# Token blocks of 512 in place of a batch's halves of 288 in the middle of a fused attention and two-layer chain

## The chip, the cores and the metric

The kernel runs on one core of a Trainium2 chip. The metric is the device time of one execution in microseconds (us), lower is better. TensorE (PE) multiplies, VectorE (DVE), ScalarE (ACT) and GpSimd (POOL) work elementwise, and SyncE (SP) issues the transfers. Every matmul is preceded by a load of its stationary operand, which the profile shows on a row of its own (PEld).

## What is computed

Four batches of eight heads attend over 576 tokens with a window of 128 and a bias that falls with distance; the result, 2304 tokens of width 512, goes through two layers:

```python
scores = scale * np.matmul(q, k.transpose(0, 1, 3, 2))
scores = np.where(mask, scores + bias[None], -1000000000.0)
attn = np.exp(scores - np.max(scores, axis=-1, keepdims=True))
attn = attn / (np.sum(attn, axis=-1, keepdims=True) + 1e-09)
x = np.matmul(attn, v)                  # as 2304 x 512
h = (x @ w1) * (x @ w2) @ w3            # w1, w2: 512 x 1024, w3: 1024 x 1024
y = h @ w_out                           # 1024 x 512
h = y @ w_in                            # 512 x 2048
out = (h * np.clip(h + 3.0, 0.0, 6.0) / 6.0) @ w_out2   # 2048 x 512
```

## The kernel before, in words

Every large product is made of three matmuls (`mm3`, lines 46 to 48): each operand is split into a high and a low part, and high by high, high by low and low by high are summed in PSUM. `split` (L74 on ACT, L75 on the engine given) makes the parts.

**Attention.** Heads go in 16 pairs `n`, four to a batch. A pair is cut into six slots (`attn_slot`): `products` (L144, the tile `s`), `scores` (L168 on DVE, L177 on ACT), `normalize` (L185, L186 on DVE, L193 on POOL), `pt` (L217, L221: transpositions of the probabilities `pr`), `pv` (L238, the tile `X`), then `x_parts`, which copies X to `xf` (L245) and splits it into `xh` and `xl`. There are two sets of `qw`, `kw`, `vw` and of four `pr` tiles, used by pairs in turn, so that a pair's loads (L113, L114, L117, all on SP's queue) come up to two pairs ahead.

**ab and y.** w3 and w_out are multiplied into one matrix W during the first 100 us. Then the tokens of a batch `b` go in two halves `s` of 288: eight `ab_unit` (f = 0 to 7; two PSUM banks, 12 triples of matmuls in all for w1 and w2, `asb` copied by ACT at L467, multiplied by DVE at L470, split into `g`), and four `y_unit` (d = 0 to 3; 8 triples over f). A half's 12 units are 8 x 24 + 4 x 24 = 288 matmuls, each 288 columns wide. y's halves are the two token halves of a scheme that needs fewer products: `y_unit` stores seven combinations to DRAM (`yT`, L489): Y11, Y21, Y22 and the differences t1 to t4.

Slots of attention are put between the units: after unit number `done` the slots up to `nslot + done + 3` have been issued. A scheduler that simulates the engines sets the final order from this program order; instructions in `keep_in_program_order` stay where they are.

**h and o.** In three blocks `j` of 384 token pairs, eight weight pairs `p` each: `h_pair` makes seven products (384 columns wide), gates them (`gate`: L659, L660, L74, L75) into `g2` tiles, and `o_jobs` adds four groups of three o matmuls (512 wide) into six PSUM banks. After the last weight pair the banks are copied out (L734 on ACT, L736 on DVE) and stored (L527). Since a block of 384 isn't a multiple of 288, `rows` cuts a 128-token store at the border of a half: 24 stores in all.

**Pools.** `xpool`, `wpool`, `sp` and `gp` lie in that order on the left side of SBUF and are closed at the end of y; `vA`, `vL`, `r2` and `g2p` then take their room. On the right, attention's tiles give way to `dec` (raw words of weights, two buffers), `vR` and `yrp` (three buffers for y read back).

The second layer's weights come as packed words, are unpacked and split on ACT and DVE (`va_make`, `vo_make`), stored to DRAM (`vad`, `vod`) and fetched again in later blocks. The first six are made during the last batch (`AT`), at whose end y's seven combinations for j = 0 are read back (`y_load`) and split (`y_split`).

Of the kernel before, what the change touches and what calls it, by code (L numbers as in the profile page):

```python
# [22 lines left out]
def tile_attention_moe_moe2(ctx: ExitStack, tc: tile.TileContext, qT, kT, vm, vt, wo, w3, w12, w2x, out):  # L23
# [56 lines left out]
    relm = cpool.tile([P, 2 * P], F32, name="relm")  # L80
# [15 lines left out]
    a1 = apool_ctx.enter_context(tc.tile_pool(name="a1", bufs=1, side="right"))  # L96
    raw_ctx = ExitStack()
# [6 lines left out]
    qw = [a1.tile([P, S + P - TAIL], F32, name=f"qw{i}") for i in range(2)]  # L104
    kw = [a1.tile([P, S], F32, name=f"kw{i}") for i in range(2)]
    vw = [a1.tile([P, NC, P], F32, name=f"vw{i}") for i in range(2)]
    rel8 = a1.tile([P, H, 2 * P], BF16, name="rel8")
    prt = [a1.tile([P, 2 * P], F32, name=f"prt{i}") for i in range(2)]

    def load_hp(n, names):  # L110
        for nm in names:
            if nm == "v":
                nc.sync.dma_start(out=vw[n % 2][:, 0 : NC - 1, :], in_=vm[n])  # L113
                nc.sync.dma_start(out=vw[n % 2][0:TAIL, NC - 1, :], in_=vt[n])  # L114
            else:
                r, src = (qw, qT) if nm == "q" else (kw, kT)
                nc.sync.dma_start(out=r[n % 2][:, 0:S], in_=src[n])  # L117
# [34 lines left out]
    def scores(n, j):  # L152
# [9 lines left out]
        pr = prt[n % 2] if tail else a1.tile([P, 2, 2 * P], F32, tag=f"pr{n % 2}", bufs=4, name=f"pr_{n}_{j}")  # L162
# [66 lines left out]
    def pv(n):  # L229
# [14 lines left out]
        x = a1.tile([P, S], F32, tag="xf", name=f"xf_{n}")  # L244
        nc.scalar.copy(x, X[:, 0:S])  # L245
        x_parts(n, x)

    def x_parts(n, x):
        xs[n] = []
        for s in range(2):  # L250
            nb = NP + 1 if s == 0 else 2 * NP - 1
            xh = xpool.tile([P, HS], F32R, tag=f"xh{s}", bufs=nb, name=f"xh_{n}_{s}")
            xl = xpool.tile([P, HS], F32R, tag=f"xl{s}", bufs=nb, name=f"xl_{n}_{s}")
            split(xh, xl, x[:, s * HS : (s + 1) * HS], nc.vector if n == NP - 1 else nc.gpsimd)
            xs[n].append((xh, xl))
# [3 lines left out]
    def attn_slot(g):  # L259
# [12 lines left out]
        if s == 1:  # L272
            normalize(n, (0, 1))
            if 0 < n < NHP - 1:
                load_hp(n + 1, "v")
# [180 lines left out]
    def ab_unit(b, s, f):  # L456
        pss = []
        hi, lo = wsp[f]
        for k in range(2):
            ps = bank(b, f"ab{k}_{b}_{s}_{f}")  # L460
            for c in range(KD):
                xh, xl = xs[b * NP + c][s]
                mm3(ps[:, 0:HS], hi[:, k * KD + c, :], lo[:, k * KD + c, :], xh, xl, c == 0, c == KD - 1)
            pss.append(ps)
            if k == 0:
                asb = xpool.tile([P, HS], F32, tag="asb", bufs=2, name=f"asb_{b}_{s}_{f}")
                nc.scalar.copy(asb, ps[:, 0:HS])  # L467
        g = gp.tile([P, 2, HS], F32R, tag="g", name=f"g_{b}_{s}_{f}")
        gh, gl = g[:, 0, :], g[:, 1, :]
        nc.vector.tensor_tensor(out=asb, in0=pss[1][:, 0:HS], in1=asb, op=ALU.mult)  # L470
        split(gh, gl, asb, nc.vector)
        gt[b, s, f] = (gh, gl)
# [4 lines left out]
    def y_unit(b, s, d):  # L477
        ds_ = slice(d * P, (d + 1) * P)
        ps = bank(b, f"y_{b}_{s}_{d}")
        for f in range(KF):  # L480
            gh, gl = gt[b, s, f]
            mm3(ps[:, 0:HS], W["h"][:, f, ds_], W["l"][:, f, ds_], gh, gl, f == 0, f == KF - 1)
        ci = d % 2

        def new(tag):
            return sp.tile([P, HS], F32, tag=tag, bufs=1, name=f"{tag}_{b}_{s}_{d}")

        def put(t, k):
            nc.sync.dma_start(out=yT[ci, k, :, b * HS : (b + 1) * HS], in_=t)  # L489

        if s == 0:
            ys[d] = new(f"y0{d}")
            nc.scalar.copy(ys[d], ps[:, 0:HS])
            put(ys[d], Y11 if d < 2 else Y21)
        elif d < 2:
            ys["t", ci] = new(f"t1{ci}")
            nc.vector.tensor_tensor(out=ys["t", ci], in0=ps[:, 0:HS], in1=ys[ci], op=ALU.subtract)
            put(ys["t", ci], YT1)
        else:
            y22, t2, t3, t4 = (new(t) for t in ("y22", "t2", "t3", "t4"))  # L500
            nc.scalar.copy(y22, ps[:, 0:HS])  # L501
            put(y22, Y22)
            nc.vector.tensor_tensor(out=t2, in0=y22, in1=ys["t", ci], op=ALU.subtract)
            put(t2, YT2)
            nc.vector.tensor_tensor(out=t3, in0=t2, in1=ys[ci], op=ALU.subtract)
            put(t3, YT3)
            nc.vector.tensor_tensor(out=t4, in0=t2, in1=ys[d], op=ALU.subtract)
            put(t4, YT4)
# [11 lines left out]
    place = {p: n for n, p in enumerate(FIRST)}  # L520
# [46 lines left out]

    yraw = {}
    yc = {}

    def y_load(j, i):
        k = PRODUCTS[i][1]
        yraw[j, i] = yrp.tile([P, 2, TH], F32, tag="yr", name=f"yraw{j}_{k}")
        dma(yraw[j, i], yT[:, k, :, j * TH : (j + 1) * TH].rearrange("c p t -> p c t"))

    def y_split(j, i):
# [5 lines left out]
        if i + 3 < len(PRODUCTS):  # L582
# [3 lines left out]
    units = []  # L586
    for s in range(2):
        units += [("ab", s, f) for f in range(KF)] + [("y", s, d) for d in range(KD)]
    g = nslot
    for b in range(B):  # L590
        if b == B - 1:
# [6 lines left out]
            yrp = ctx.enter_context(tc.tile_pool(name="yrp", bufs=3, side="right"))  # L598
# [249 lines left out]
```

## Time and profile before

| what | value |
|---|---|
| time, median of 3 runs | 874.26 us (871.99 to 876.93) |
| the profiled execution's own time | 873.87 us |
| its span, first to last instruction | 872.1 us |
| PE busy | 847.9 us (97%), 5264 matmuls |
| PEld busy | 744.3 us (85%) |
| DVE, ACT, POOL busy | 462.8, 383.6, 97.9 us |
| granted TensorE clock | 0.999 of full speed |

The span has four stages: up to about 101 us the first batch's attention and W; 101 to 386 us ab and y with the attention of the other batches between them; 386 to 484 us ab and y alone, with decoding on ACT and DVE; from 484 us h and o. Spans of matmuls overlap, since they are pipelined: how fast they go is read from the distance of their starts.

### The profile page before, as it was taken

The numbers are of one execution on the slowest core, as the hardware profiler recorded it, in microseconds if no ns is written. First come the engines' busy times: TensorE is split into PE (matmuls) and PEld (weight loads), VectorE is DVE, ScalarE is ACT, GpSimd is POOL, SyncE is SP. The second block draws the span as 40 slices with busy tenths as digits, with TensorE's granted clock in tenths as the row PEclk, the third lists the DMA queues.
The fourth block names the chain that finished last, engine by engine and source line by source line (L and its number), as shares of the span: only waits on it lengthen the run. The fifth ranks groups of instructions, "written<-read, shape, count | busy, mean of one in ns | idle before, by whom it ended". The sixth has DMA issues, their size and how long they took to land.

```text
span 872.1 us, 13688 instructions
## 1 busy us (share of the span) xinstructions
PE 847.9 (97%) x5264; PEld 744.3 (85%) x5264; DVE 462.8 (53%) x1074; ACT 383.6 (44%) x859; POOL 97.9 (11%) x188
## 2 busy tenths in 40 slices
PE   5999999999999999999999899999999999999997
PEld 3454699899898989999999888989889888898886
DVE  5896652444414444232667787786644346443443
ACT  6676653443424344331555454554433235332322
POOL 3314222220222222020000000000000000000000
PEclk9999999999999999999999999999999999999999
DMA  9973211112101120006477779569865558645402
GB/s 362 362 289 133 90 42 62 49 42 96 52 33 41 54 96 15 28 1 219 172 277 269 271 259 361 200 250 381 297 248 200 199 196 308 225 176 223 181 1 72
DMA packets 37393, 148.99 MB, mean 171 GB/s; under 512 B 4049, under 2 KB 17617, under 8 KB 26065
## 3 DMA queue, kind: packets, MB, share of 16 engines
q1 hardware_dynamic: 37328, 148.13, 46.8%
q8 instruction: 41, 0.67, 0.3%
q14 instruction: 24, 0.19, 0.1%
HBM read 112.07 MB, written 36.04 MB: 170 GB/s over the span
## 4 chain that ended last, share of the span: by engine, by line
PE 90%; DVE 4%; DMA 3%; issue 1%; POOL 1%; ACT 1%; SPq 0%; DVEq 0%; POOLq 0%; ACTq 0%
PE ab L46 8%; PE o L46 8%; PE o L47 8%; PE o L48 7%; PE ab L47 7%; PE ab L48 7%; PE wps L350 7%; PE h L46 7%; PE h L47 6%; PE h L48 6%; PE y L46 4%; PE y L47 4%; PE y L48 4%; PE X L238 3%; PE pt L217 3%; PE s L144 2%
## 5 line engine op out<-in xcount | busy, mean ns | idle before, releaser
L46 PE MATMUL ab<-xh,w12h 128*128 128x288 f32 x512 | 156.4, 306 | 0.4 <-ACT y L501 0.3
L47 PE MATMUL ab<-xl,w12h 128*128 128x288 f32 x512 | 151.2, 295 | 0.0
L48 PE MATMUL ab<-xh,w12l 128*128 128x288 f32 x512 | 150.8, 295 | 0.0
L46 PE MATMUL h<-yhi,va 128*128 128x384 f32 x336 | 114.2, 340 | 1.4 <-issue 1.1
L46 PE MATMUL o<-vo,g 128*128 128x512 f32 x288 | 113.1, 393 | 1.4 <-ACT g L74 1.4
L47 PE MATMUL h<-ylo,va 128*128 128x384 f32 x336 | 113.3, 337 | 0.8 <-DVE ylo L75 0.8
L48 PE MATMUL h<-yhi,va 128*128 128x384 f32 x336 | 113.2, 337 | 0.0
L47 PE MATMUL o<-vo,g 128*128 128x512 f32 x288 | 113.1, 393 | 0.0
L46 PEld LDWEIGHTS ab<-xh,w12h 128*128 128x128 f32 x512 | 96.2, 188 | 9.1 <-issue 6.5
L47 PEld LDWEIGHTS ab<-xl,w12h 128*128 128x128 f32 x512 | 96.6, 189 | 0.2 <-issue 0.2
L48 PEld LDWEIGHTS ab<-xh,w12l 128*128 128x128 f32 x512 | 96.4, 188 | 0.0
L48 PE MATMUL o<-vo,g 128*128 128x512 f32 x288 | 86.5, 392 | 0.0
L659 ACT ACTIVATE rl<-c,three 128x384 f32<-128x384 f32 x72 | 44.2, 616 | 74.9 <-DVE c L689 43.7
L193 POOL TENSOR_SCALAR pr<-pr,rc 128x256 f32<-128x256 f32 (+1 forms) x128 | 63.3, 513 | 118.4 <-DVE rc L186 118.0
L470 DVE TENSOR_TENSOR asb<-ab,asb 128x288 f32<-128x288 f32 x64 | 29.0, 452 | 88.2 <-PE ab L48 87.0
L46 PE MATMUL y<-g,Wh 128*128 128x288 f32 x256 | 75.5, 300 | 0.0
L47 PE MATMUL y<-g,Wh 128*128 128x288 f32 x256 | 74.8, 296 | 0.0
L48 PE MATMUL y<-g,Wl 128*128 128x288 f32 x256 | 74.5, 295 | 0.0
L46 PEld LDWEIGHTS h<-yhi,va 128*128 128x128 f32 x336 | 63.1, 188 | 8.2 <-DVE rl L660 2.9
L47 PEld LDWEIGHTS h<-ylo,va 128*128 128x128 f32 x336 | 63.1, 188 | 4.8 <-DVE ylo L75 1.4
L46 PEld LDWEIGHTS o<-vo,g 128*128 128x128 f32 x288 | 54.0, 188 | 11.4 <-ACT g L74 1.7
L48 PEld LDWEIGHTS h<-yhi,va 128*128 128x128 f32 x336 | 63.0, 188 | 0.0
(92 smaller groups left out, 1413.7 us busy)
## 6 DMA issues: line engine op xcount, KB each, us to landing
va<-vad SPq DMA_DIRECT2D x18, 1792.0 KB, 7.3
vo<-vod SPq DMA_DIRECT2D x18, 1024.0 KB, 9.2
raww<-in_w_dram SPq DMA_DIRECT2D x16, 1024.0 KB, 6.9
rawv<-in_w2x_dram SPq DMA_DIRECT2D x16, 1024.0 KB, 7.8
vad<-va SPq DMA_DIRECT2D x8, 1792.0 KB, 7.9
vod<-vo SPq DMA_DIRECT2D x8, 1024.0 KB, 12.5
yraw<-yT SPq DMA_DIRECT2D x21, 384.0 KB, 9.5
qw<-in_qT_dram SPq DMA_DIRECT2D x16, 288.0 KB, 2.9
```

Source lines behind the costliest of these rows:

```text
L46: nc.tensor.matmul(ps, lh, rh, start=first, stop=False, **kw)
L47: nc.tensor.matmul(ps, lh, rl, start=False, stop=False, **kw)
L48: nc.tensor.matmul(ps, ll, rh, start=False, stop=last, **kw)
L144: in_order(not head, nc.tensor.matmul(ps[j // 2][h][:, j % 2, 0:nk], qw[n % 2][HB[h], P * j : P * (j + 1)], kw[n % 2][HB[h], k0 : k0 + nk] ...
L193: nc.gpsimd.tensor_scalar(out=o, in0=o, scalar1=rc[:, 2 * j + h : 2 * j + h + 1], scalar2=1.0, op0=ALU.mult, op1=ALU.mult)
L217: nc.tensor.transpose(p[:, o : o + P], prob[n, j][:, h, c : c + P], ident)
L238: last_pe["x", n, h] = in_order(not head, nc.tensor.matmul(X[HB[h], q0 : q0 + nq], vw[n % 2][:, kb, HB[h]], th[:, o : o + nq], start=i == ...
L350: nc.tensor.matmul(ps[:, 0:DM], w3v[i][:, m, :], wov[m], start=m == 0, stop=m == KF - 1)
L470: nc.vector.tensor_tensor(out=asb, in0=pss[1][:, 0:HS], in1=asb, op=ALU.mult)
L659: nc.scalar.activation(rl, h, AF.Relu, bias=three[:, 0:1], scale=1.0)
```

## The change

ab and y take blocks of 512 tokens whatever batch they are of: four of 512 and one of 256 (`CHUNKS`). A block's two halves (256 tokens, 128 in the last) are now the token halves of y and h, so one `y_unit` makes what two made before. `x_parts` puts a batch's pieces into the blocks that they belong to: a block's tile is filled from two batches, so four `xf` are kept. From the fifth pair on there is one set of q, k, v and `pr`: the second set lies in a pool `a2` that is closed before `gp` and `sp` are opened, whose order is swapped. Six decodes are spread over block 3's units, y is read back in block 4 through the two `dec` buffers, and `yrp` moves behind `g2p`. A 128-token store is never cut (18 stores). The last pair's o matmuls are put in an order of their own and pinned to it.

```diff
-    HS = S // 2
+    CH = 512
+    HC = CH // 2
+    CHUNKS = [CH] * (NT // CH) + [NT % CH]
...
+    for i, pool in enumerate((a1, a2)):
+        qw.append(pool.tile([P, S + P - TAIL], F32, name=f"qw{i}"))
...
+    def place(n):
+        return n % 2 if n < NP else 0
...
-        pr = prt[n % 2] if tail else a1.tile([P, 2, 2 * P], F32, tag=f"pr{n % 2}", bufs=4, name=f"pr_{n}_{j}")
+        pr = prt[place(n)] if tail else (a1, a2)[place(n)].tile(
+            [P, 2, 2 * P], F32, tag="pr", bufs=4, name=f"pr_{n}_{j}"
+        )
...
         x_parts(n, x)
+        if NP <= n < NHP - 1:
+            load_hp(n + 1, "v")
...
-            split(xh, xl, x[:, s * HS : (s + 1) * HS], nc.vector if n == NP - 1 else nc.gpsimd)
-            xs[n].append((xh, xl))
+        b, c = divmod(n, NP)
+        eng = nc.vector if n == NP - 1 else nc.gpsimd
+        t = xpool.tile([P, 2, CH], F32R, tag="x", bufs=NP + 2, name=f"x_{b}_{c}")
+        k0 = b * (S - CH)
+        split(t[:, 0, k0:CH], t[:, 1, k0:CH], x[:, 0 : CH - k0], eng)
+        if b > 0:
+            split(t[:, 0, 0:k0], t[:, 1, 0:k0], xtail[c], eng)
...
-            if n + 2 < NHP:
-                load_hp(n + 2, "q")
+            if n != NP - 1 and n + 1 < NHP:
+                load_hp(n + 1 if n >= NP else n + 2, "q")
...
-    sp = p1.enter_context(tc.tile_pool(name="sp", bufs=2))
     raw_ctx.close()
+    a2_ctx.close()
     gp = p1.enter_context(tc.tile_pool(name="gp", bufs=KF))
+    sp = p1.enter_context(tc.tile_pool(name="sp", bufs=1))
...
-    def ab_unit(b, s, f):
+    def ab_unit(k, f):
+        N = CHUNKS[k]
...
-                mm3(ps[:, 0:HS], hi[:, k * KD + c, :], lo[:, k * KD + c, :], xh, xl, c == 0, c == KD - 1)
+                mm3(ps[:, 0:N], hi[:, i * KD + c, :], lo[:, i * KD + c, :], xh, xl, c == 0, c == KD - 1)
...
-        if s == 0:
-            ys[d] = new(f"y0{d}")
-            nc.scalar.copy(ys[d], ps[:, 0:HS])
-            put(ys[d], Y11 if d < 2 else Y21)
...
+        if d < 2:
+            ys[ci] = new(f"y11{ci}")
+            nc.scalar.copy(ys[ci], ps[:, 0:M])
+            put(ys[ci], Y11)
+            ys["t", ci] = less(f"t1{ci}", ps[:, M:N], ys[ci], YT1)
         else:
+            y2 = new("y2", 2)
+            nc.scalar.copy(y2, ps[:, 0:N])
+            put(y2[:, 0:M], Y21)
+            put(y2[:, M:N], Y22)
+            t2 = less("t2", y2[:, M:N], ys["t", ci], YT2)
+            less("t3", t2, ys[ci], YT3)
+            less("t4", t2, y2[:, 0:M], YT4)
...
+        elif i % 2 == 0:
+            t = dec.tile([P, 2, 2, TH], F32, tag="raw", name=f"yraw{j}_{k}")
...
-            AT = [1, 4, 6, 8, 10, 12]
+            AT = [1, 3, 5, 7, 9, 11]
...
-            done = len(units) * b + iu + 1
+            done = 2 * (len(units) * k + iu + 1)
...
+        if n == len(units2) - 1:
+            qi = [(q, i) for q in ((0, 0), (1, 0), (1, 1)) for i in range(NTT)]
+            for i in range(NTT):
+                qi.insert(NTT * 3 - 1 + 2 * i, ((0, 1), i))
...
-                        for r0, m, t0 in rows(j, th, i):
-                            dma(out[t0 : t0 + m, :], ob[r0 : r0 + m, :])
+                    t0 = row(j, th, i)
+                    dma(out[t0 : t0 + P, :], ob)
```

PE has 3803 instructions after the change and had 4663: 864 matmuls of ab and y fewer, and nothing else but their order. Three places follow. In the names, the first number behind `s` and `pt` is the pair; `ab0_1_0` is w1's half of block 1, f = 0 (before: `ab1_0_1_6`, w2's half of batch 0, half 1, f = 6).

PE between the products of pair 8 and its first transposition, before:

```order
L144 MATMUL s_8_2_0_1860<-kw0_92,qw0_90 128x256
L46 MATMUL ab1_0_1_6_1780<-xh_0_1_305,w12h6_802 128x288
...
L46 MATMUL ab0_0_1_7_1820<-xh_3_1_741,w12h7_806 128x288
L47 MATMUL ab0_0_1_7_1820<-xl_3_1_742,w12h7_806 128x288
L48 MATMUL ab0_0_1_7_1820<-xh_3_1_741,w12l7_807 128x288
L217 MATMUL pt_8_0_2000<-ident_60,pr_8_0_1869 128x128
```

and with the change:

```order
L153 MATMUL s_8_2_0_1524<-kw0_93,qw0_92 128x256
L52 MATMUL ab0_1_0_1674<-x_1_3_1509,w12h0_498 128x512
L53 MATMUL ab0_1_0_1674<-x_1_3_1509,w12h0_498 128x512
L54 MATMUL ab0_1_0_1674<-x_1_3_1509,w12l0_499 128x512
L52 MATMUL ab1_1_0_1689<-x_1_3_1509,w12h0_498 128x512
L53 MATMUL ab1_1_0_1689<-x_1_3_1509,w12h0_498 128x512
L54 MATMUL ab1_1_0_1689<-x_1_3_1509,w12l0_499 128x512
L228 MATMUL pt_8_0_1645<-ident_60,pr_8_0_1533 128x128
```

The 24 matmuls that stood between have become six. Pair 12 has the same; in the other nine pairs from the sixth on (numbers 5 to 15) 24 to 28 wide matmuls stand there.

ACT where y ends and h begins, with the semaphores that an instruction waits for (DMAHW: a transfer), before:

```order
L501 COPY y22_3_1_3_5218<-y_3_1_3_5193 128x288 [waits DMAHW0_49,DVE_49,PE_49]
L672 COPY s1_0_0_5257<-h_0_0_0_5250 128x384 [waits PE_49]
L63 ACTIVATE rawv2_6_4764<-rawv2_6_4764 128x1024 [waits DMAHW3_49]
L659 ACTIVATE rl_0_0_5292<-h_0_0_0_5250,three_62 128x384 [waits PE_49]
...
L74 CAST g2_0_0_00_5293<-rl_0_0_5292 128x384 [waits DMAHW5_49,DMAHW3_49,DMAHW6_49,DMAHW2_49,DMAHW7_49,DMAHW1_49,DMAHW0_49]
```

and with the change:

```order
L531 COPY y2_4_3_4123<-y_4_3_4098 128x256 [waits DMAHW4_49,DVE_49,DMAHW5_49,PE_49,Activation_49]
L710 COPY s1_0_0_4166<-h_0_0_0_4159 128x384 [waits PE_49]
L65 ACTIVATE rawv2_6_3990<-rawv2_6_3990 128x1024
L697 ACTIVATE rl_0_0_4201<-h_0_0_0_4159,three_61 128x384 [waits PE_49]
...
L76 CAST g2_0_0_00_4202<-rl_0_0_4201 128x384 [waits DVE_49]
```

The first gated tile no longer waits for any transfer; y's last copy still does.

PE at the very end, before (the rest of the last group):

```order
L47 MATMUL o_2_5_7576<-vo23_8138,g2_2_7_01_8368 128x512
L48 MATMUL o_2_3_7556<-vo23_8138,g2_2_7_01_8368 128x512
L48 MATMUL o_2_4_7572<-vo23_8138,g2_2_7_01_8368 128x512
L48 MATMUL o_2_5_7576<-vo23_8138,g2_2_7_01_8368 128x512
```

and with the change, PE and then what DVE has left from the gate of `01` on:

```order
L54 MATMUL o_2_3_6461<-vo23_7043,g2_2_7_01_7273 128x512
...
L54 MATMUL o_2_4_6477<-vo23_7043,g2_2_7_01_7273 128x512
L52 MATMUL o_2_5_6481<-vo23_7043,g2_2_7_01_7273 128x512
L53 MATMUL o_2_5_6481<-vo23_7043,g2_2_7_01_7273 128x512
L54 MATMUL o_2_5_6481<-vo23_7043,g2_2_7_01_7273 128x512
```

```order
L738 TENSOR_TENSOR c12_2_7_7270<-h_2_7_2_7222,u2_2_7_7185 128x384
L777 TENSOR_SCALAR ob_2_0_7293<-o_2_1_6444 128x512
L698 SCALAR_TENSOR_TENSOR rl_2_7_7272<-rl_2_7_7272,c12_2_7_7270 128x384
L77 TENSOR_TENSOR g2_2_7_01_7273<-rl_2_7_7272,g2_2_7_01_7273 128x384
L777 TENSOR_SCALAR ob_2_1_7315<-o_2_4_6477 128x512
```

Three banks used to end within three matmuls of each other; now the last three end nine, three and no matmuls before PE's end, and the first three well ahead of them. One of DVE's copies stands between two steps of the last gate.

## Rows read from the trace of the kernel before

**Rows 1.** The page: PE's busy time, and the chain that ended last by engine.

```profile
PE 847.9 (97%) x5264; PEld 744.3 (85%) x5264; DVE 462.8 (53%) x1074; ACT 383.6 (44%) x859; POOL 97.9 (11%) x188
...
PE 90%; DVE 4%; DMA 3%; issue 1%; POOL 1%; ACT 1%; SPq 0%; DVEq 0%; POOLq 0%; ACTq 0%
```

**Rows 2.** Windows: stretch, length, busy and (matmuls) by engine, clock, DMA share, GB/s.

```profile
101.00:386.00 285.00, 282.61 (x2276) 263.83 (x2275) 112.29 (x399) 121.30 (x367) 62.02 (x121) 1.00 0.16 50
...
440.00:460.00 20.00, 20.00 (x152) 20.00 (x151) 12.38 (x19) 11.05 (x18) 0.00 (x0) 1.00 0.75 277
484.20:500.00 15.80, 13.30 (x73) 12.35 (x72) 12.77 (x25) 8.22 (x14) 0.00 (x0) 1.00 0.83 299
```

**Rows 3.** The chain in pieces (start, us, what): o, h, transpositions and products.

```profile
183.83 2.04 PE s L144 x20
...
197.67 0.77 PE pt L217 x7
...
751.56 0.17 PE h L46
...
753.66 0.23 PE o L46
...
860.07 0.23 PE o L46
...
865.55 0.24 PE o L48
```

**Rows 4.** Timeline of PE: one transposition within ab (start, length).

```profile
188.95 0.30 PE L48 MATMUL ab<-xh,w12l 128*128 128x288 f32 x1
189.08 0.27 PE L217 MATMUL pt<-ident,pr 128*128 128x128 f32 x1
...
189.33 0.29 PE L47 MATMUL ab<-xl,w12h 128*128 128x288 f32 x1
```

**Rows 5.** PE's waits, 101 to 386 us (total, times, longest).

```profile
PE pt L217 <- POOL pr L193: 2.4, 5, 0.5
```

**Rows 6.** Timeline from a pair's products to its first normalised tile.

```profile
183.76 2.12 PE L144 MATMUL s<-kw,qw 64*128 64x192 f32 x20
...
187.96 0.18 DVE L186 RECIPROCAL rc<-rc 128x4 f32<-128x4 f32 x1
188.34 1.17 POOL L193 TENSOR_SCALAR pr<-pr,rc 128x128 f32<-128x128 f32 x3 [5.78 <-DVE rc L186]
```

**Rows 7.** Groups by line and form, and the transfers' landing: normalising, q, y's read.

```profile
L193 POOL TENSOR_SCALAR pr<-pr,rc 128x128 f32<-128x128 f32 x32 | 13.8, 444 | 89.5 <-DVE rc L186 89.5
...
yraw<-yT SPq DMA_DIRECT2D x21, 384.0 KB, 9.5
qw<-in_qT_dram SPq DMA_DIRECT2D x16, 288.0 KB, 2.9
```

**Rows 8.** Start of h: waits from 484.2 to 500 us.

```profile
ACT g L74 <- DMA yT<-t: 2.9, 1, 2.9
...
PE o L46 <- ACT g L74: 1.4, 1, 1.4
...
PE h L46 <- issue: 1.1, 1, 1.1
```

**Rows 9.** Start of h on DVE's timeline, and the chain's piece there.

```profile
489.19 1.23 DVE L68 SCALAR_TENSOR_TENSOR rawv<-rawv 128x1024 int32<-128x1024 int32 x1
490.33 0.55 DVE L660 SCALAR_TENSOR_TENSOR rl<-rl,h 128x384 f32<-128x384 f32 x1
...
488.06 9.16 DMA yT<-t
```

**Rows 10.** The end: timeline from 863.9 us, and the last eight stores' landing.

```profile
864.40 3.95 SPq L527 DMA_DIRECT2D out_dram<-ob  x8
...
865.39 0.84 PE L48 MATMUL o<-vo,g 128*128 128x512 f32 x3
865.82 1.29 DVE L736 TENSOR_SCALAR ob<-o 128x512 f32<-128x512 f32 x2 [1.12 <-PE o L48]
866.04 0.60 ACT L734 ACTIVATE ob<-o 128x512 f32<-128x512 f32 x1 [1.18 <-PE o L48]
...
DMA to landing us min/median/max: 2.0/2.9/3.3
```

**Rows 11.** The chain from 600 to 620 us: one read of y.

```profile
617.08 3.33 DMA yraw<-yT
```

More of the change, by code (lines that the diff above doesn't have):

```diff
@@ L464, in ab_unit @@
             pss.append(ps)
[L465 to L472, printed above, removed]
+            if i == 0:
+                asb = xpool.tile([P, CH], F32, tag="asb", bufs=2, name=f"asb_{k}_{f}")
+                nc.scalar.copy(asb[:, 0:N], ps[:, 0:N])
@@ L474, in tile_attention_moe_moe2, with y_unit @@
+        g = gp.tile([P, 2, CH], F32R, tag="g", name=f"g_{k}_{f}")
+        gh, gl = g[:, 0, 0:N], g[:, 1, 0:N]
+        nc.vector.tensor_tensor(out=asb[:, 0:N], in0=pss[1][:, 0:N], in1=asb[:, 0:N], op=ALU.mult)
+        split(gh, gl, asb[:, 0:N], nc.vector)
+        gt[k, f] = (gh, gl)
     Y11, YT1, Y21, Y22, YT3, YT2, YT4 = range(7)
     ys = {}
-    def y_unit(b, s, d):
+    def y_unit(k, d):
+        N = CHUNKS[k]
+        M = N // 2
         ds_ = slice(d * P, (d + 1) * P)
-        ps = bank(b, f"y_{b}_{s}_{d}")
+        ps = bank(k, f"y_{k}_{d}")
@@ L480, in y_unit @@
         for f in range(KF):
-            gh, gl = gt[b, s, f]
-            mm3(ps[:, 0:HS], W["h"][:, f, ds_], W["l"][:, f, ds_], gh, gl, f == 0, f == KF - 1)
+            gh, gl = gt[k, f]
+            mm3(ps[:, 0:N], W["h"][:, f, ds_], W["l"][:, f, ds_], gh, gl, f == 0, f == KF - 1)
         ci = d % 2
[L485 to L489, printed above, removed]
@@ L491, in y_unit, with new @@
-        if s == 0:
-            ys[d] = new(f"y0{d}")
-            nc.scalar.copy(ys[d], ps[:, 0:HS])
-            put(ys[d], Y11 if d < 2 else Y21)
[L495 to L498, printed above, removed]
-        else:
[L500 to L508, printed above, removed]
+        def new(tag, n=1):
+            return sp.tile([P, n * HC], F32, tag=tag, name=f"{tag}_{k}_{d}")[:, 0 : n * M]
@@ L519, in tile_attention_moe_moe2 @@
     units2 = [(j, p) for j in range(NBLK) for p in ORDER[j]]
-    place = {p: n for n, p in enumerate(FIRST)}
+    place2 = {p: n for n, p in enumerate(FIRST)}
     va = {}
@@ L566, in store @@
             dma(dst, f32(t))
+    yrp = []
     yraw = {}
@@ L572, in y_load @@
         k = PRODUCTS[i][1]
-        yraw[j, i] = yrp.tile([P, 2, TH], F32, tag="yr", name=f"yraw{j}_{k}")
+        if j > 0:
+            yraw[j, i] = yrp[0].tile([P, 2, TH], F32, tag="yr", name=f"yraw{j}_{k}")
+        elif i % 2 == 0:
+            t = dec.tile([P, 2, 2, TH], F32, tag="raw", name=f"yraw{j}_{k}")
+            for m in range(2):
+                yraw[j, i + m] = t[:, m, :, :]
         dma(yraw[j, i], yT[:, k, :, j * TH : (j + 1) * TH].rearrange("c p t -> p c t"))
@@ L703, in h_pair, with row @@
         return gs
-    def rows(j, th, i):
-        c, end = j * TH + i * P, j * TH + (i + 1) * P
-        while c < end:
-            m = min(end, (c // HS + 1) * HS) - c
-            yield c - j * TH - i * P, m, c // HS * S + th * HS + c % HS
-            c += m
+    def row(j, th, i):
+        c = j * TH + i * P
+        k, c = divmod(c, HC)
+        return k * CH + th * CHUNKS[k] // 2 + c
     def o_jobs(j, n, gs):
```

150 lines of the change are left out of this document (84 added, 66 removed).

## The prediction

> **What bounds the kernel now.** I read the page first [rows 1]: PE is busy for 97% of the span, and 90% of the chain that ended last runs through it, while no other engine passes 53%. So the time moves by what PE itself does, by the few microseconds in which it waits, and by what lies behind its last matmul. The windows [rows 2] split that by stage: PE is full from 101 to 386 us and in a stretch of ab alone (152 matmuls in 20 us), and falls to 13.30 of 15.80 us only at the start of h. The granted clock reads 1.00 in all three, the 2.4 GHz level, so no part of the change can gain by the clock; it could only lose by longer pauses, which I don't foresee. Then I took the distance of matmul starts from the chain and the timeline, the waits by stage, and the two ends of the second half (start of h, end of o).
>
> The profiled execution took 873.87 us, of which the span is 872.1; the median of the runs is 874.26, 0.4 above. The sum is made against 873.87. Half a per cent, 4.4 us, is about what a measurement of this kernel can tell from no change: faster is below 869.9, slower above 878.6.
>
> **1. The stream of ab and y.** Before there are 8 halves of 288 matmuls, 2304 with 288 columns; each starts 20.00/152 = 131.6 ns behind the one ahead [rows 2]. With the change there are 4 x 288 = 1152 of 512 columns and 288 of 256, the same columns in 864 fewer matmuls. What 512 columns cost, o shows: the chain has 25 of its matmuls from 860.07 to 865.55 + 0.24 us, 5.72/25 = 228.8 ns [rows 3]. The line through both widths is 0.434 ns a column and 6.6 ns a matmul. It gives 173 ns at 384 columns, where h has 12 matmuls from 751.56 to 753.66 us [rows 3], 175 ns; so I trust it down to 256: 117.7 ns. Before: 2304 x 131.6 = 303.2 us. After: 1152 x 228.8 + 288 x 117.7 = 263.6 + 33.9 = 297.5. That is **-5.7 us**. Bounds: 256 columns as dear as 288 makes the last term 37.9 and the gain 1.7; as cheap as one of seven transpositions in bulk (0.77/7 = 110 ns, [rows 3]) makes it 7.9. I take the line, since a third width lies on it.
>
> The Trainium skill, "TensorE: Matmul & The Clock Gate", section "Back-to-back issue gap", gives for single warm matmuls columns/2.4 + 2.5 ns; by that the change saves 864 x 2.5 = 2.2 us, near rival B. The same section's sustained figures, 81 ns at 128 columns and 131 at 512, would leave 64 ns a matmul whatever its width, an estimate of 55 us saved; here 512 columns take 228.8 ns, so the trace disagrees and that case gets no chance.
>
> **2. Fewer cuts in the stream.** Attention now stands between 60 wider units rather than 96. One transposition put between two ab matmuls moves the next one from 2 x 131.6 = 263 ns to 380 ns (188.95 to 189.33 us, [rows 4]), 0.12 us, against 0.11 in bulk [rows 3]. A cut costs nothing: **0**.
>
> **3. Waits of attention.** Before, PE waits five times for normalised probabilities, 2.4 us in all [rows 5]. From a pair's first product to its first normalised tile pass 188.34 - 183.76 = 4.58 us [rows 6] and one multiplication, 0.44 [rows 7]: 5.0 us. What PE has to do meanwhile is the 20 products, 2.04 us [rows 3], and the matmuls between, whose numbers are in the order shown in the section on the change. In nine of the pairs 5 to 15 these are at least 24: 2.04 + 24 x 0.229 = 7.5 us, so no wait. In pairs 8 and 12 they are six: 2.04 + 1.37 = 3.4, so PE waits 1.6 us twice. 3.2 - 2.4 = **+0.8**. Bounds: -2.4, if the scheduler's estimate is right and none waits, and +4, if both wait twice as long.
>
> **4. One set of q, k, v and pr.** q, k and v of the next pair are now asked for only when the pair's own use has ended; q lands 2.9 us after its issue [rows 7], and the pair's next products are two units of 24 wide matmuls (5.5 us each) or more behind, so I cost it at **0**. Without that cover (SP's queue held up: v waits there for the X of the pair ahead, and q, k and y's stores stand behind it) it would be some 3 us in each of 11 pairs, 33 us at worst; I take 0, as the nearest row is the 2.9. The single set of pr ties a pair's scores to the transpositions of the pair ahead, which are a unit or more earlier.
>
> **5. Wider evictions.** ACT's and DVE's copies grow from 288 to 512 columns; a 512-wide one took 0.60 us on ACT and some 0.65 on DVE [rows 10]. An ab bank has 12 matmuls, 2.7 us, of the other bank for cover: **0**. If the cover were gone at each of 60 units, 0.6 x 60 = 36 us; nothing points there.
>
> **6. y read back in block 4.** Two raw buffers are refilled and split in turn, so a load has two units of 24 matmuls with 256 columns, 2 x 24 x 0.1177 = 5.65 us, before its split. One read landed in 3.33 us on the chain [rows 11]; the median of all is 9.5 [rows 7]. I take **0**, since in the order on SP the stores of decoded weights now come behind y's last; the other end is rival E.
>
> **7. Start of h.** PE idles 15.80 - 13.30 = 2.5 us there [rows 2]: 1.1 for h's banks and 1.4 for ACT's first gated tile [rows 8]. ACT's part was itself a wait of 2.9 us for a store of y, `yT<-t`, which took 9.16 us to land [rows 8, 9]: `g2` lies where y's store buffers lay. With the pools swapped the order shows that ACT's cast waits for DVE alone, so the 1.4 goes. The 1.1 stays: DVE has a decode of 1.23 us ahead of `rl` [rows 9] in both orders. What is late next is y's last copy on ACT, which still waits for a store; PE needs ACT some 4 us later only. **-1.4**, between -2.5 (both gone) and +0.5 (that copy late).
>
> **8. The end.** The last matmul ends at 865.39 + 0.84 = 866.23 us, the span at 872.1. Between lie copies of the last three banks, two on DVE in a row (until 867.11) and one on ACT, eight stores on SP until 868.35 and a landing of 2.0 to 3.3 us [rows 10]. With the change one ACT copy and one store are left behind the last matmul. ACT's copy of 0.60 us in place of DVE's two, 1.29, takes 0.7 off, and the store that was eighth in the queue now goes as it is ready: some 0.5 more, with each issue 3.95/8 = 0.5 us. Against this stands DVE's extra copy between two steps of the last gate, up to 0.3 us for PE. In all **-1.2**, from -2.0 (SP's issue free as well) to -0.3 (the gate late, the landing slow).
>
> Sum: -5.7 + 0.8 - 1.4 - 1.2 = -7.5; 873.87 - 7.5 = **866.4 us**.
>
> **The rivals.**
> A is the forecast.
> B: the stream gains 1.7 only, since 256 columns cost what 288 do. Time 866.4 + 4.0 = 870.4. For it: of the widths below 288 the trace has no such stream. Against it: transpositions of 128 columns run at 110 ns [rows 3].
> C: no wait in pairs 8 and 12, since the shorter chain through six matmuls lets the engines pass: 866.4 - 3.2 = 863.2. For it: five waits before were 0.5 at most [rows 5]. Against: 5.0 us from product to tile.
> D, the other sign: with one set the chain from the products to the first normalised tile gets longer, because q or k lands late or 512-wide evictions of ab stand between scores on DVE and ACT. It decides once it passes the 7.5 us that PE has to do in the nine other pairs. At 9.1 us each of those waits 1.6, 9 x 1.6 = 14.4, and the time is 880.8; slower than 878.6 begins at 8.9 us. Against it: 2.5 us of room, and POOL, ACT and DVE are busy for less than half of 101 to 386 us [rows 2].
> E: y's reads take the median 9.5 us in block 4. Three refills late by 9.5 - 5.65 = 3.85 each make 11.6; two units that stand ahead of the first read's use, 5.65, take a share: +6.0, 872.4.
> F: another wait takes the place of the 1.4 at the start of h, such as y's last copy behind its store: 867.8.
> That the change doesn't do what it says can't well be: the order lists the 1152 and 288 matmuls.
>
> **How the numbers follow.** A .55, almost all of it faster (.53, same .02); B .12 (.04 faster, .08 same); C .12 (faster); D .05 (slower); E .08 (.02, .05, .01); F .08 (.07, .01). Together faster .78, same .16, slower .06. The range goes from 861.0 (C, with 2.2 more if 256 columns are as cheap as the bound) to 871.5 (B's 870.4 and 1.1 of the open ends of 7 and 8); left out are D, most of E and the tail below, some 2 in 10.
>
> **What will show it.** In the profile of the changed kernel: ab and y in full stretches 229 ns apart in blocks 0 to 3 and 118 in block 4 (130 there: B). PE waiting for POOL's `pr` in two places, 1.6 us each (none: C; in most pairs: D, with q, k or DVE named). At the start of h the cast on ACT not waiting for a transfer, and PE idle 1.1 us there rather than 2.5. In block 4 no wait for `yraw` (E). From the last matmul to the end of the span 4.6 to 5 us rather than 5.9. The forecast is wrong if PE's busy time falls by less than 4 us, or if its idle time grows from the 24 us that it is now by more than 3.

## The result and the profile after

The changed kernel takes **864.73 us** (median of 4 runs, 864.09 to 865.27); the kernel before, in runs on the same chip, 874.71. The ratio is 0.9887, 95% interval 0.9857 to 0.9917: 1.1% faster. The forecast was 866.4, with a range of 861.0 to 871.5. The profiled execution's span is 862.3 us, where it was 872.1.

The first part of the page and its chain, after, against [rows 1]:

```profile
PE 837.9 (97%) x4400; PEld 684.5 (79%) x4400; DVE 455.3 (53%) x1030; ACT 378.1 (44%) x810; POOL 101.3 (12%) x189
...
PE 90%; DVE 3%; DMA 3%; ACT 2%; issue 1%; SPq 0%; POOL 0%; DVEq 0%; POOLq 0%; ACTq 0%
```

PE is the bound as before, with 4400 matmuls for 5264, 864 fewer (the section on the change counts 3803 and 4663 instructions, 860 apart; the traces have these). Its busy time falls by 10.0 us, its idle time stays (24.4 us for 24.2). Its waits, first from 101 to 472 us, then from 472 to 520, then in the rest (total, times, longest; against [rows 5] and [rows 8]):

```profile
PE pt L228 <- POOL pr L204: 2.6, 2, 1.3
PE ab L52 <- ACT asb L492: 0.5, 1, 0.5
...
PE h L52 <- DVE rl L698: 2.4, 2, 1.3
...
PE h L52 <- ACT yhi L76: 0.7, 1, 0.7
PE h L53 <- DVE ylo L77: 0.6, 1, 0.6
PE h L52 <- DVE u L722: 0.3, 1, 0.3
```

The five waits for `pr` have become two of 1.3 us. At the start of h no wait names ACT's `g`. DVE's `rl` has two waits: one of 1.0 us, which takes the place of the 1.1 us of [rows 8], and a new one 31 us later:

```profile
513.60 0.45 PE L52 MATMUL h<-yhi,va 128*128 128x384 f32 x1 [1.35 <-DVE rl L698]
```

The stream, on PE's timeline: the first and the last of 23 matmuls of 512 columns in a row.

```profile
106.87 0.39 PE L53 MATMUL ab<-x,w12h 128*128 128x512 f32 x1
...
111.89 0.39 PE L54 MATMUL ab<-x,w12l 128*128 128x512 f32 x1
```

That is 5.02/22 = 228.2 ns. Over all undisturbed distances of starts the means are 228.0 ns at 512 columns, 120.0 at 256 and, in the kernel before, 132.8 at 288 (2128 distances). The 131.6 of the forecast came from 152 starts in 20 us [rows 2]; such a count takes in a piece at each border. The same count on the new kernel has 90 starts between 400 and 420 us, 222 ns, below 228.2 in the same way.

Going through PE's records from first to last gives where the 9.8 us of the spans come from:

| stage | before | after | difference |
|---|---|---|---|
| to the first matmul of ab | 101.42 | 102.93 | +1.51 |
| matmuls of ab and y, with what follows each | 315.87 | 307.75 | -8.12 |
| attention's pieces between them | 66.19 | 64.64 | -1.55 |
| h and o | 382.75 | 383.16 | +0.41 |
| end of the last matmul to end of the span | 5.86 | 3.83 | -2.03 |

The first line I take as chance, which no run settles: PE has the same 391 matmuls there, and over the profiles of this study, of either kernel, ab began between 101.1 and 104.3 us. The end, on the timeline (PE, DVE and ACT), against [rows 10]:

```profile
857.84 0.69 DVE L777 TENSOR_SCALAR ob<-o 128x512 f32<-128x512 f32 x1 [1.97 <-PE o L54]
857.87 0.39 PE L53 MATMUL o<-vo,g 128*128 128x512 f32 x1
...
858.09 0.39 PE L54 MATMUL o<-vo,g 128*128 128x512 f32 x1
858.52 0.60 ACT L775 ACTIVATE ob<-o 128x512 f32<-128x512 f32 x1 [1.46 <-PE o L54]
```

One copy of 0.60 us and its store stand behind the last matmul; DVE's copy of the bank before ends with that matmul.

### The profile page after: what moved, and what is told of

Read it like the earlier page. It is cut to its first block, busy times and chain, and to the rows that moved or that the text cites. A ratio compares the mean times of both kernels' runs of the same rounds, so it can differ in the third digit from the quotient of the medians.

```text
span 862.3 us, 11832 instructions
## 1 busy us (share of the span) xinstructions
PE 837.9 (97%) x4400; PEld 684.5 (79%) x4400; DVE 455.3 (53%) x1030; ACT 378.1 (44%) x810; POOL 101.3 (12%) x189
## 4 chain that ended last, share of the span: by engine, by line
PE 90%; DVE 3%; DMA 3%; ACT 2%; issue 1%; SPq 0%; POOL 0%; DVEq 0%; POOLq 0%; ACTq 0%
PE ab L52 8%; PE ab L53 8%; PE ab L54 7%; PE o L53 7%; PE o L54 7%; PE o L52 7%; PE wps L373 7%; PE h L52 6%; PE h L53 6%; PE h L54 6%; PE y L52 4%; PE y L53 4%; PE y L54 4%; PE X L249 4%; PE s L153 3%; PE pt L228 3%
## 5 line engine op out<-in xcount | busy, mean ns | idle before, releaser
L52 PE MATMUL ab<-x,w12h 128*128 128x512 f32 (+1 forms) x320 | 120.1, 377 | 0.6 <-ACT asb L492 0.5
L53 PE MATMUL ab<-x,w12h 128*128 128x512 f32 (+1 forms) x320 | 118.9, 372 | 0.0
L54 PE MATMUL ab<-x,w12l 128*128 128x512 f32 (+1 forms) x320 | 118.2, 369 | 0.0
L204 POOL TENSOR_SCALAR pr<-pr,rc 128x256 f32<-128x256 f32 (+1 forms) x128 | 66.3, 536 | 131.1 <-DVE rc L197 119.4
L52 PEld LDWEIGHTS ab<-x,w12h 128*128 128x128 f32 x320 | 60.3, 189 | 14.3 <-issue 3.1
L53 PEld LDWEIGHTS ab<-x,w12h 128*128 128x128 f32 x320 | 60.4, 189 | 11.8 <-issue 2.7
L54 PEld LDWEIGHTS ab<-x,w12l 128*128 128x128 f32 x320 | 60.4, 189 | 10.0
L54 PEld LDWEIGHTS o<-vo,g 128*128 128x128 f32 x288 | 53.9, 188 | 10.8 <-DVE g L77 0.3
L495 DVE TENSOR_TENSOR asb<-ab,asb 128x512 f32<-128x512 f32 (+1 forms) x40 | 25.4, 636 | 69.5 <-PE ab L54 57.0
L77 DVE TENSOR_TENSOR g<-rl,g 128x384 fp32r<-128x384 f32 x96 | 53.0, 555 | 17.0 <-ACT g L76 14.6
L188 ACT ACTIVATE pr<-pr,mn 128x256 f32<-128x256 f32 (+1 forms) x128 | 59.9, 469 | 4.6 <-DVE mn L179 3.4
L52 PEld LDWEIGHTS o<-vo,g 128*128 128x128 f32 x288 | 54.0, 188 | 9.6 <-ACT g L76 0.2
```

The lines of the kernel that those rows point to most:

```text
L52: in_order(pinned, nc.tensor.matmul(ps, lh, rh, start=first, stop=False, **kw))
L53: in_order(pinned, nc.tensor.matmul(ps, lh, rl, start=False, stop=False, **kw))
L54: in_order(pinned, nc.tensor.matmul(ps, ll, rh, start=False, stop=last, **kw))
L77: lo_eng.tensor_tensor(out=lo, in0=src, in1=f32(hi), op=ALU.subtract)
L188: nc.scalar.activation(o, o, AF.Exp, bias=mn[:, col : col + 1], scale=-1.0, accum_out=sm[:, col : col + 1])
L204: nc.gpsimd.tensor_scalar(out=o, in0=o, scalar1=rc[:, 2 * j + h : 2 * j + h + 1], scalar2=1.0, op0=ALU.mult, op1=ALU.mult)
```

## The experiments

Each edit is to the changed kernel, unless it says otherwise. For each run I give the median, and from its profile the time from the first matmul of ab to the end of the last matmul of o ("middle", 764.81 us before, 755.55 after) and from there to the end of the span ("end", 5.86 before, 3.83 after). The runs were made on three chips. Each ratio is against the kernel before on the same chip, so runs of different chips are compared by their ratios; the changed kernel's are 0.9887 and 0.9892.

**The changed kernel again.** 

> The changed kernel as it is, as a base for the others on this chip. Theory (fewer matmuls with the same columns, one bank behind the last matmul): 864 to 866 us, 9 to 10 below the kernel before. Rival (the gain was luck of the runs): 868 or more.

Measured: 865.2 us, ratio 0.9892 (0.9876 to 0.9909); middle 757.70, end 3.82. The gain repeats. The profile is 2.15 us longer in the middle than the first one though the program is the same, and 1.6 of it arise at one place. Windows of the two around pair 12, the first changed kernel's, then this one's (length, busy and count by engine, clock):

```profile
290.00:292.00 2.00, 0.82 (x4) 0.35 (x2) 1.48 (x10) 2.00 (x10) 0.29 (x1) 1.00 0.82 249
292.00:294.00 2.00, 1.33 (x5) 1.00 (x6) 0.96 (x3) 1.75 (x6) 1.33 (x4) 1.00 0.12 46
294.00:295.60 1.60, 1.60 (x8) 1.31 (x7) 0.83 (x1) 0.33 (x1) 1.43 (x3) 1.00 0.03 10
295.60:299.00 3.40, 3.40 (x18) 2.70 (x17) 0.00 (x0) 0.59 (x1) 1.24 (x3) 1.00 0.00 0
```

```profile
292.00:294.00 2.00, 0.56 (x2) 0.14 (x1) 0.88 (x6) 2.00 (x9) 0.89 (x3) 1.00 0.75 279
294.00:295.60 1.60, 1.19 (x5) 1.02 (x6) 0.96 (x3) 1.35 (x4) 0.77 (x3) 1.00 0.00 0
295.60:299.00 3.40, 3.40 (x12) 2.58 (x10) 0.82 (x1) 0.29 (x2) 2.64 (x5) 0.52 0.02 5
```

Both have the pause in which PE waits for `pr`. In the second the granted clock then reads 0.52, the 1.2 GHz level (the "half clock" below), for 3.4 us, and 12 matmuls run where 18 did. Of six profiles with PE's order of the change at this place, four show it.

**Two matmuls of 256 columns for each of 512.**

```diff
-mm3(ps[:, 0:N], hi[...], lo[...], xh, xl, c == 0, c == KD - 1)
+for a in range(0, N, HC):
+    z = slice(a, a + HC)
+    mm3(ps[:, z], hi[...], lo[...], xh[:, z], xl[:, z], c == 0, c == KD - 1, ...)
```

and so in y. Each half starts its own sum in the bank, so the sums of ab and y are not kept whole; instructions and sizes are as said.

> The changed kernel with every matmul of ab and y in blocks 0 to 3 cut into two of 256 columns into the same bank: 1152 matmuls more, the same banks, copies and places of attention. Theory (the stream's gain is a fixed part of each matmul): 1152 x (2 x 119.6 - 228.0 ns) = 12.9 us slower than the changed kernel, some 877.5 us, and more than undone by it is the whole change. Rival (the gain comes from fewer pieces and wider copies, and matmuls of 256 run at half the time of 512): 0 to 2 us slower.

Measured: 872.6 us (ratio 0.9981, 0.9969 to 0.9993); middle 763.53. PE's timeline of this kernel, the first and the last of 36 matmuls in a row:

```profile
404.80 0.28 PE L52 MATMUL ab<-x,w12h 128*128 128x256 f32 x1
...
409.00 0.28 PE L54 MATMUL ab<-x,w12l 128*128 128x256 f32 x1
```

4.20/35 = 120.0 ns, so two halves cost 240 ns where the whole costs 228. With the mean of 119.9 the stream is 2304 x 119.9 - 1152 x 228.0 = 13.6 us longer. The time rose by less than expected, in part because attention's places were not the same: the scheduler put 70 halves between the products and transpositions of pairs 8 and 12, so the waits of 3.1 us went. 13.6 - 3.1 leaves 10.5; from the first ab to the first h the profile is 9.1 us longer, and 1.4 us stay unexplained. The fixed part of a matmul is shown; the rival (2 us at most) falls.

**The old order at the end** (the list `qi`, `pinned` and the share of copies as before).

> The changed kernel with the order of the last o matmuls and the copies as before. Theory: the stretch from the last matmul to the end of the span goes back from 3.8 us to 5.7 to 6.1, the time is 1.5 to 2.2 us above the changed kernel. Rival (the end was short by a quick last store, not by the order): the stretch stays below 4.5 us, the time within 0.5 us.

Measured: 864.65 us, ratio 0.9883 (0.9865 to 0.9902); middle 754.56, end 4.77. Both expectations miss the end, which is 0.94 longer. The middle is 1.0 shorter, and the time is the same, as only the rival has it. What the middle won is seen in PE's waits of this kernel at the ends of h's first two blocks:

```profile
PE h L53 <- DVE ylo L77: 0.8, 2, 0.6
```

0.8 us, where the change has 1.6 with ACT's `yhi` and DVE's `u`.

**That order alone, on the kernel before** (with the change's share of copies at the last end).

> The kernel before with the change's order of the last 36 o matmuls alone; the eight stores at the end stay eight, the copies at the other ends stay. Theory (of the 2.05 us that the end lost, 0.9 to 1.0 are the order and 1.1 the two stores fewer): from the last matmul to the end of the span 4.9 us in place of 5.9, time 0.9 us below the kernel before. Rival (the stores queue at SP, so the order only helps where there are six): 5.6 us or more, no change in time.

Measured: 872.78 us, ratio 0.9974 (0.9963 to 0.9986); end 3.80. Its last matmuls and copy on the timeline:

```profile
865.91 0.39 PE L51 MATMUL o<-vo,g 128*128 128x512 f32 x1
...
866.14 0.40 PE L52 MATMUL o<-vo,g 128*128 128x512 f32 x1
866.57 0.60 ACT L740 ACTIVATE ob<-o 128x512 f32<-128x512 f32 x1 [1.50 <-PE o L52]
```

Both expectations miss: the order takes 2.1 us off by itself, with eight stores, where 0.9 was expected. So the two gains don't add: six stores with the old order give 4.77, eight with the new one 3.80, both 3.83. PE pays nothing for the order (h and o take 382.5 us, 382.75 before).

**The share of copies as before at the ends of h's first two blocks.**

```diff
-if i % 2 == 0:
+if (i if n == len(units2) - 1 else o) % 2 == 0:
```

> The changed kernel with the banks at the ends of h's first two blocks copied out as before, three on ACT and three on DVE in turn, and the new order at the last end only. Theory (the new share, four on ACT, delays ACT's split of y for the next block): PE's waits at those ends fall from 1.6 to 0.8 us, 0.8 us faster than the changed kernel; the last matmul to the end of the span stays 3.8 us. Rival (these waits are chance): no change in them.

Measured: 864.57 us, ratio 0.9892 (0.9872 to 0.9911); end 3.83, waits there 1.1 us (0.8 on `ylo`, 0.3 on `yhi`). Some 0.5 of the 0.8 us that were expected; in the time it can't be told from nothing.

**The pools as before.**

```diff
-gp = ...tile_pool(name="gp", bufs=KF)
 sp = ...tile_pool(name="sp", bufs=1)
+gp = ...tile_pool(name="gp", bufs=KF)
```

> The changed kernel with y's store buffers again below the g tiles, so that the first gated tile lies on them and ACT's first cast of it waits for their transfers. Forecast's step (the swap takes a wait of 1.4 us away): 1.4 us slower, PE waits for ACT's g at the first o. Rival (the transfers land before DVE has that tile's rl ready, at some 7.5 us into h, so the swap takes nothing away): within 0.4 us of the changed kernel, PE's waits at the start of h still on DVE's rl, 2.4 us.

Measured: 864.48 us, ratio 0.9879 (0.9864 to 0.9895); middle 755.74, with the half clock at pair 12. PE's only wait from 472 to 520 us:

```profile
PE h L52 <- DVE rl L698: 1.0, 1, 1.0
```

No wait on `g` comes back, although in this kernel's order ACT's cast again waits for eight transfers. They have landed by then: the last of y's stores lands at 484.03 us, 0.2 us before DVE has that tile's `rl` ready, at 484.25. So the swap takes nothing away, and the reason that the forecast gave falls. What differs from the kernel before is SP's queue. There y's last three stores stood behind a store of decoded weights (`vad`, 1792 KB; SP's timeline, and the landing of the three):

```profile
485.83 0.42 SPq L527 DMA_DIRECT2D vad<-va  x1
486.35 2.14 SPq L489 DMA_DIRECT2D yT<-t  x3
...
DMA to landing us min/median/max: 9.2/9.6/10.1
```

Here, as in the change, they stand ahead of it (the landing is that of the last five):

```profile
478.39 1.77 SPq L516 DMA_DIRECT2D yT<-t  x3
480.21 0.48 SPq L555 DMA_DIRECT2D vad<-va  x1
...
DMA to landing us min/median/max: 4.3/5.3/5.8
```

They are also smaller, 64 KB for 144; no run separates the two.

That the second wait on `rl` is missing here was not expected. In the change it lies at 513.60 us, behind a word of weights that lands 13.0 us after its issue (the chain of the changed kernel, start and length):

```profile
495.48 13.02 DMA rawv<-in_w2x_dram
```

Here the same transfer takes 10.5 us, where four other profiles with the change's order at this place have 13.0 to 13.3; why, stays open.

**The decode at the start of h later.**

```diff
-if k in (1, 4) and todo:
+if k in ((4,) if n == 0 else (1, 4)) and todo:
```

> The changed kernel with the decode of the first weight pair of h moved from behind the second product to behind the fifth, so that DVE has no decode ahead of the first rl. Theory (PE's 2.4 us of waits at the start of h are that decode, 0.68 + 1.23 us, standing ahead of rl): 1.5 to 2.4 us faster than the changed kernel, the waits on rl below 0.5 us. Rival (DVE is full for 17 us there, the order doesn't matter): the waits move to another instruction of DVE, time within 0.5 us.

In the changed kernel DVE and PE stand like this (timeline of all engines, from 480 us):

```profile
480.25 0.68 DVE L66 TENSOR_SCALAR rawv<-rawv 128x1024 int32<-128x1024 int32 x1
...
481.04 1.23 DVE L70 SCALAR_TENSOR_TENSOR rawv<-rawv 128x1024 int32<-128x1024 int32 x1
...
482.19 0.55 DVE L698 SCALAR_TENSOR_TENSOR rl<-rl,h 128x384 f32<-128x384 f32 x1
...
482.79 0.44 PE L52 MATMUL h<-yhi,va 128*128 128x384 f32 x1 [1.02 <-DVE rl L698]
```

Measured: 863.46 us, ratio 0.9871 (0.9853 to 0.9888); from the first h on 2.3 us shorter than the change (380.84 for 383.16). PE's waits from 472 to 520 us:

```profile
PE h L52 <- DVE rl L698: 0.2, 1, 0.2
```

As the theory said, the waits go but for 0.2 us, the one at 513.60 us too. DVE is as full as before (31.4 of the first 40 us of h in both); it is the order on it that PE waits for. In the time it is not beyond doubt: against 0.9892 on the same chip the intervals overlap.

**Later transpositions in pairs 8 and 12** (`issue_after` on the last matmul of the next ab unit).

> The changed kernel with the first transposition of pairs 8 and 12 put behind 24 more matmuls of ab (30 after the products in place of 6). Theory (PE reaches it 1.3 us before POOL has the tile, and the copy of an ab bank is late by 0.5 us behind it; the pause then brings 3 to 4 us at the 1.2 GHz level in some executions): the waits of 2.6 and 0.5 us go, the granted clock stays at 1.00 around pair 12, 2.6 to 4.7 us faster. Rival (the pair's chain is as long as the way to X, so the wait moves to X): within 1 us.

Measured: 865.67 us, ratio 0.9902 (0.9882 to 0.9922); middle 757.01. From 101 to 472 us PE now has one wait:

```profile
PE ab L52 <- ACT asb L494: 3.9, 2, 2.2
```

The wait moved, though not to X: ab's bank is free only when ACT has copied it, and that copy stands behind the pair's exponentials. Nor did the granted clock stay at 1.00: behind the pause of 2.2 us at pair 12 it is at the 1.2 GHz level from 293.0 to 296.4 us. Leaving PE more to do doesn't help where the work needs the engine that is late.

**Earlier products instead.**

```diff
-in_order(not head, nc.tensor.matmul(
+last_pe["s", n] = in_order(not head, nc.tensor.matmul(
...
+behind = last_pe.get(("s", {1: 2 * NP, 2: 3 * NP}.get(k))) if (f, i) == (0, 1) else None
+with tc.issue_after(behind.ins) if behind else nullcontext():
     mm3(ps[:, 0:N], ...)
```

> The changed kernel with the nine first matmuls of the second ab bank of blocks 1 and 2 put behind the products of pairs 8 and 12 instead of ahead of them: 15 matmuls of ab between products and first transposition in place of 6, and the products 2 us earlier, so that ACT's exponentials start earlier too. Theory (the chain from products to the first tile takes 4.7 us, and PE has 2.0 + 15 x 0.228 = 5.5 us): the waits of 2.6 and 0.5 us on POOL's pr and ACT's copy fall below 0.8 us in all, no half clock around pair 12, 2.3 to 4.7 us from products' block to h. Rival (as when the transposition was only put later: ACT's copies of the ab banks stand behind nine exponentials whatever PE does): 2 us or more of waits on that copy.

Measured: **861.13 us**, ratio 0.9844 (0.9828 to 0.9859). From 101 to 472 us PE has no wait left, and around pair 12 the window reads

```profile
280.00:300.00 20.00, 19.88 (x120) 15.20 (x119) 9.03 (x33) 9.74 (x28) 5.88 (x11) 1.00 0.25 78
```

against 111 matmuls in the first profile of the change and 99 or 100 in those with the half clock. From the first ab to the first h it takes 369.33 us, for 372.39 without and 373.98 with the half clock: 3.1 and 4.6 us less, the waits of 2.6 and 0.5 and, in the second case, 1.6 of clock.

The profiled execution is this run's slowest (863.58 us): in it the clock falls elsewhere, at the end of h's first block, behind waits of 0.3, 0.7 and 0.6 us that the change has too (the window there, granted clock 0.50). From the first h on it is 1.7 us longer than the change's first profile (384.88 for 383.16).

```profile
612.40:615.80 3.40, 3.27 (x10) 3.27 (x11) 2.28 (x6) 1.02 (x2) 0.00 (x0) 0.50 0.95 361
```

**q and k later.** From the sixth pair on ACT issues them behind its copy of X.

```diff
+cp = nc.scalar.copy(x, X[:, 0:S])
+if NP < n < NHP - 1:
+    with tc.issue_after(cp.ins):
+        nc.scalar.dma_start(out=qw[0][:, 0:S], in_=qT[n + 1])
+        nc.scalar.dma_start(out=kw[0][:, 0:S], in_=kT[n + 1])
...
-if n != NP - 1 and n + 1 < NHP:
+if n != NP - 1 and n <= NP:
     load_hp(n + 1 if n >= NP else n + 2, "q")
```

k's load on SP's queue ends in the same way, so the edit moves these loads to another queue as well as later.

> The changed kernel with q and k of the next pair asked for only behind the copy of X, on ACT's queue, from the sixth pair on, some two thirds of a pair later than in the changed kernel. Theory (one set of q, k, v costs nothing, since q lands 2.9 us after its issue and 8 us of matmuls stand between): no wait of PE for q or k, and a time within 2.5 us of the changed kernel, below rather than above it, since the order now has 18 matmuls in pairs 8 and 12. Rival (one set is tight): PE waits for q or k in most pairs, 10 us or more.

Measured: 881.54 us, ratio 1.0091 (1.0065 to 1.0117); in the profile, which took 876.58 and is the fastest of four, the middle is 768.72, 13.2 us longer than the change's. PE's largest waits from 101 to 472 us:

```profile
PE pt L228 <- POOL pr L204: 3.4, 7, 0.9
PE ab L52 <- ACT x L76: 3.1, 2, 1.6
PE X L249 <- DVE th L238: 1.6, 2, 0.8
PE s L153 <- DMA kw<-in_kT_dram: 1.2, 1, 1.2
```

Both expectations miss. Only one wait is for k, yet by the ratios the kernel is 2% slower than the change: most pairs' products come 13 matmuls or more later, the last pair of a batch runs out of ab and y to stand beside, and the next block waits for its `x`. These places are around 195, 285 to 296 and 384 to 392 us. The other three executions took 880.7 to 883.0 us at a mean granted clock of 0.983 to 0.988, for 0.997 in the profile, so part of what they lose beyond it may be the clock.

**Three edits together** (earlier products, later decode, old share of copies).

> Three edits together: the order of the run above at pairs 8 and 12, the decode behind the fifth product at the start of h, and the old share of copies at the ends of h's first two blocks. If the waits add up: 2.5 + 2.2 + 0.5 below the changed kernel, and up to 1.6 more where its clock had fallen: 858.5 to 860.5 us, faster than both kernels. Rival (one engine's work that is late comes back as another's wait): 862 or more.

Measured: **858.08 us** (857.16 to 859.13), ratio 0.9808 (0.9792 to 0.9825); middle 749.54. By the ratios that is 0.8% below the change, and the time is just below the range expected. The middle is 6.0 us shorter than in the change's first profile, and PE's waits behind 101 us are 5.8 us less:

```profile
PE h L52 <- DVE rl L700: 0.2, 1, 0.2
PE h L53 <- DVE ylo L77: 0.8, 2, 0.6
PE h L52 <- ACT yhi L76: 0.3, 1, 0.3
```

The waits add up, since each lay in a stretch of its own.

## Why the forecast held, step by step

1. **The stream**, -5.7: right in kind, too small. By the distances measured it is 2304 x 132.8 - 1152 x 228.0 - 288 x 120.0 = 306.0 - 262.7 - 34.6 = 8.7 us. The mis-sized factor is the 131.6 for 288 columns; 1.2 ns by 2304 matmuls is 2.8 of the 3.0 us. The bound of -7.9 was passed for the same reason. The widths of 288 and 512 now lie on 0.425 ns a column and some 10.4 ns a matmul (256 columns: 119.2, measured 120.0), and halving the matmuls shows the fixed part directly. The Trainium skill, "TensorE: Matmul & The Clock Gate", section "Back-to-back issue gap", has 215.8 and 109.2 ns for 512 and 256 columns by its formula for single matmuls: the slope agrees, the fixed part is four times its 2.5 ns here. Rival B falls.
2. **Cuts**, 0: nearly. The first matmul behind a piece of attention takes some 225 ns to the next start where 133 is usual before, some 325 for 228 after, some 0.1 us that the lone transposition of [rows 4] didn't show; 14 pieces fewer (52 for 66) would be worth about a microsecond. Beyond the stream's 8.7, ab, y and attention together gained 1.0 us, with waits 0.4 longer.
3. **Waits of attention**, +0.8: the two places and nearly the size (2 x 1.3 for 2 x 1.6). The chain is the 5.0 us of the forecast; what was put too small is PE's work meanwhile, 3.7 us rather than 3.4, since the first of the six matmuls behind the products takes 0.34 us to the next start and the last one runs its 0.39. PE at pair 8 in the change:

```profile
195.09 2.11 PE L153 MATMUL s<-kw,qw 64*128 64x192 f32 x20
...
198.40 0.39 PE L54 MATMUL ab<-x,w12l 128*128 128x512 f32 x1
200.10 0.33 PE L228 MATMUL pt<-ident,pr 128*128 128x128 f32 x1 [1.31 <-POOL pr L204]
```

Not foreseen: ACT's copy 0.5 us late behind it, and the half clock that the pause can bring, 1.6 us. The run with earlier products shows all three. Rival C falls.

4. **One set of q, k, v**, 0: no wait names them in the change. But "some 3 us in each of 11 pairs" was the wrong price for the lost cover, and two units of matmuls the wrong measure of it. The run with later loads lost 2% with 1.2 us of waits for k. Rival D's sign was right for such a case, its place (nine pairs waiting for tiles) was not.
5. **Wider copies**, 0, and 6. **reads of y**, 0: held but for the 0.5 us above; no wait names `yraw`, so rival E falls.
7. **Start of h**, -1.4: this step failed. In the stretch of [rows 8] what was forecast came: no wait on `g`, and 1.0 us of idle time left. But the pool swap didn't do it, since with the old pool order the same transfers land in time; the forecast took the place of `g` for the cause, and what differs is when y's last stores land. And the sum had no term for the second wait on `rl`, 1.35 us at 513.60 us, behind a late word of weights and its decode on DVE: the 2.5 us [rows 8] became 2.4. Rival F has the size of that, not the place. A later decode takes all but 0.2 us of both waits away.
8. **The end**, -1.2: right in kind; it is -2.03. The last store goes out 0.66 us behind the last matmul rather than 1.70, and lands in 2.13 us rather than 3.12; the sum had no term for a faster landing. The bound of -2.0 was meant for a queue that costs nothing, and it was just passed. The order does it alone. What the new share of copies gave back, some 0.5 us of waits at the ends of h's earlier blocks by the run with the old share, the forecast didn't look for.

The sum came out near in part by luck, because errors stood against each other. The stream was too small by 3.0 us, attention with its cuts by 1.8 (-1.0 where +0.8 was forecast) and the end by 0.8; on the other side h and o are 0.4 longer, not 1.4 shorter, and in the profile ab began 1.5 us late.

## What to carry to other kernels

Where PE is full, count its instructions: the same columns in fewer matmuls are worth the fixed part of each, and that is to be read from distances between starts, not from a count in a window. Before a wait on a transfer is booked as gained by a new place in memory, look at when the transfer lands in the new order: here the wait went with the old place too. Then look at what the engine behind it does later, where a wait of the same size can come up. Where PE waits behind a long chain, start the chain earlier rather than giving PE more to do that needs the same engines, and measure a load's slack by what the whole pair's delay costs, not by its landing time.

## What the runs showed of the hardware

A pause of PE can cost more than its length. At pair 12 PE waits 1.3 and 0.5 us, and in four of six profiles the granted clock then falls from 1.00 to the 1.2 GHz level (0.52 in the window shown) for 3.4 us, 1.6 us lost; in the other two it stays at 1.00, as it does in all six behind the 1.3 us alone at pair 8. It also fell behind one pause of 2.2 us at pair 12 (the run with later transpositions) and, in one profile, behind 0.3, 0.7 and 0.6 us at the end of h's first block (0.50 from 612.4 to 615.8 us). Where the pauses at pairs 8 and 12 are gone the clock holds at 1.00 from 101 to 380 us. The lower level is also seen between 10 and 23 us in five of the thirteen profiles, where PE is half busy at first (4.45 of the 10 us from 10 to 20 us in the change); in the others the record of the clock begins only at some 20 us. What it costs there can't be told apart from the transfers.
